# Fused recurrence and two expert mixtures: low parts of the first mixture's weights by an accumulating transfer

## The chip, the cores and the metric

The kernel runs on one core of a Trainium2 chip. Its engines work side by side: TensorE (PE in the profile; PEld is its weight load), VectorE (DVE), ScalarE (ACT), GpSimd (POOL) and SyncE (SP, which issues most transfers). The metric is the device time in microseconds (us), the median of several runs. For the kernel before it is 1308.95 us (three runs, 1308.48 to 1310.84).

## What is computed

```python
def reference(**kwargs):
    attn_out = _attn_ref(**attn_kwargs)          # a gated linear recurrence over 2 x 5056 tokens of 256
    x = attn_out.reshape(B * S, D)               # 10112 tokens
    x = _moe_ref(x=x, **moe_kwargs)              # first mixture
    return _moe2_ref(x=x, **moe2_kwargs)         # second mixture

def _moe_ref(x, w_gate, w1, w2):                 # 8 experts, each takes exactly N // 8 = 1264 tokens
    ...                                          # pairs (token, expert) taken greedily by their logit
    for e in range(E):
        mask = assigned == e
        h = np.maximum(x[mask] @ w1[e], 0.0)     # 256 -> 1024
        out[mask] = h @ w2[e]                    # 1024 -> 256

def _moe2_ref(x, expert_emb, tau, w1, w2):       # 8 experts, each token goes to its best one
    ...
        out[mask] = gate_w[mask, None] * (h @ w2[e])
```

The matrix products are done in a short float format (`fp32r`). So that the result is precise enough, each operand is split into a high part (the value rounded to that format) and a low part (the value minus its high part), and each product is the sum of three: high by high, high by low, low by high.

## The kernel before

**Stages.** The recurrence fills the first 180 us or so. The first mixture follows, to about 800 us: eight *phases*, one for each expert in the order in which the greedy assignment fills them. The second mixture takes the rest, in blocks of 512 and 256 tokens.

**A phase** has five chunks of up to 256 tokens and four *steps* for each chunk, so 20 steps. A step is `g1` (first layer for two of the eight groups of 128 hidden units, PE lines L1125) and, two steps later, `g2` (second layer, L1157 to L1159). Between them ACT writes the high part `hh` (L1130) and DVE the low part `hl` (L1131). Each chunk's tokens come by two GpSimd indirect transfers, the gathers `xg` (L1092), and PE turns them (`L1100`) before ACT and DVE split them.

**Work beside the steps of a phase** prepares the next one: the *selection* of the next expert and its tokens, a long chain of small DVE operations with a few on ACT and PE. Two of its places matter here. `lists` (L943 to L970) turns the chosen tokens into a list of numbers: DVE writes `om` (L953), `oh` (L957), `lo` (L959) and `rh` (L960, L961), then PE does 24 small products (L966), and from their result come the numbers `ids` that the gathers use. The search for the cut uses `KY` (L222, turned on PE at L769) and counts `scm` on ACT (L794). POOL also adds third parts of results (L1201) and stores rows by indirect transfers (`x2r`, L1266).

**The weights** of the next phase come as four raw tiles of 128x1024 numbers (512 KB each, issued by SP). `split_weights` makes of each a high part on ACT (L1055) and a low part: where `low[k]` is V, by one DVE subtraction (L1057), where it is G, by four POOL subtractions of 128x256 (L1063). Phase 0 has V four times, phase 1 has V, G, V, G, phases 2 to 7 have G four times, the first block of the second mixture has G, V, G, V, all later blocks have V.

**What sets the order.** Every engine works through its own instructions in the order in which the program wrote them. That order comes from a planner, the class `Flow`: each job is a generator that yields a cost for each engine (`{"A": 0.95, "G": 2.6}`) and a delay. The planner keeps a clock for each engine and writes a job's next piece when, by these costs, its engine will be free. PE sets the pace. `fl.until(...)` runs the planner until a job is done by its clock. A changed cost therefore moves instructions of all engines, in the whole first mixture.

Of the kernel before, what the change touches and what calls it, by code (L numbers as in the profile page):

```python
# [9 lines left out]
F32 = mybir.dt.float32  # L10
# [3 lines left out]
AF = mybir.ActivationFunctionType  # L14
ALU = mybir.AluOpType
# [5 lines left out]
D = 256  # L21
# [33 lines left out]
W_FIRST = 5.0  # L55
# [26 lines left out]
def build(tc, x, r_gate, i_gate, a_param, w_gate, w1, w2, emb, tau, v1, v2, out):  # L82
    nc = tc.nc
    V, A, G, T, SP = nc.vector, nc.scalar, nc.gpsimd, nc.tensor, nc.sync
# [4 lines left out]
    def ct(name, shape, dt=F32):  # L89
        return cp.tile(shape, dt, name=name)  # L90
# [122 lines left out]
    fl = Flow()  # L213
# [204 lines left out]
    low, top = ct("low", [P, 1]), ct("top", [P, 1])  # L418
# [623 lines left out]
    def split_weights(raw, low, wt, first=0.0, each=0.0):  # L1042

        wt.update({n: wp.tile([P, 2, F], F32R, name=n) for n in ("w1h", "w1l")})
        wt.update({n: wp.tile([P, NF, D], F32R, name=n) for n in ("w2h", "w2l")})
        for k in range(4):
            while len(raw) <= k:
                yield {}, 0.1
            yield {"A": 0.95, **({"G": 2.6} if low[k] is G else {"V": 1.13})}, each if k else first
            if k < 2:  # L1050
                src, h, l = raw[k], wt["w1h"][:, k], wt["w1l"][:, k]
            else:
                src = raw[k].rearrange("p (f d) -> p f d", d=D)
                h, l = (wt[n][:, 4 * k - 8:4 * k - 4, :D] for n in ("w2h", "w2l"))
            A.activation(h, src, AF.Copy)  # L1055
            if low[k] is V:
                V.tensor_tensor(out=l, in0=src, in1=h.bitcast(F32), op=ALU.subtract)  # L1057
                continue

            for q in range(4):  # L1060
                at = slice(q * D, (q + 1) * D)
                p = (lambda t: t[:, at]) if k < 2 else lambda t: t[:, q]
                G.tensor_tensor(out=p(l), in0=p(src), in1=p(h.bitcast(F32)), op=ALU.subtract)  # L1063


    base = ct("base", [P, E])
# [6 lines left out]
    st = {ph: dict(x={}, xg=[], w={}) for ph in range(E)}  # L1073
# [9 lines left out]
    def gather(ph, c):  # L1083
        o = st[ph]
        ids = sel[ph]["ids"]
        t0, n = CHUNKS[c]
        xg = room(o, "xg", [P, 2, D], bufs=XG)
        o["xg"].append(xg)
        for j in range((n + P - 1) // P):
            yield dict(G=1.04), 0  # L1090
            k = t0 // P + j
            G.indirect_dma_start(out=xg[:, j], out_offset=None, in_=x1,  # L1092
                                 in_offset=bass.IndirectOffsetOnAxis(ap=ids[:, k:k + 1], axis=0),
                                 bounds_check=N - 1, oob_is_err=False)
        yield {}, 3.0
# [176 lines left out]
    def load_of(ph):  # L1272
        e = nc.values_load(sel[ph]["ei"], engines=[ENG.SP], min_val=0, max_val=E - 1,
                           skip_runtime_bounds_check_because="one of the eight experts")
        st[ph]["raw"] = []
        return load_weights(st[ph]["raw"], w1, w2, e)
# [5 lines left out]
    fl.until(("lists", 0))  # L1282
    t = fl.free["PE"]
    sp0 = split_weights(st[0]["raw"], [V, V, V, V], st[0]["w"])
    drain(gather(0, 0))
    fl.done.add(("g", 0, 0))
# [14 lines left out]
    def poll(ph, u):  # L1301

        nonlocal loaded
        for p in range(2, E):
            if p <= ph + 2 and ("ei", p - 1) in fl.done and ("sel", p) not in chain:
                chain["sel", p] = 1
                fl.add(PRIO_SEL, ("sel", p), select(p, sp, pm))
        p = ph + 1
        if p < E:
            if ("ei", p) in fl.done and ("w", p - 1) in fl.done and loaded < p:  # L1310
                loaded = p
                fl.add(2, ("load", p), load_of(p))
            if loaded == p and u >= 2 and ("w", p) not in chain:
                chain["w", p] = 1
                fl.add(4, ("w", p), split_weights(st[p]["raw"], [V, G, V, G] if p == 1 else [G, G, G, G], st[p]["w"], W_FIRST))
            if ("lists", p) in fl.done:
                for c in range(NCH):

                    k = c + NCH - XG
                    if ("g", p, c) not in chain and (k < 0 or ("x", ph, k) in fl.done) and (c == 0 or ("g", p, c - 1) in chain):  # L1320
                        chain["g", p, c] = 1
                        fl.add(4 if c > 0 else 2.5, ("g", p, c), gather(p, c))

        if ("base", E - 2) in fl.done and "early" not in chain:
            chain["early"] = 1
            fl.add(1, "early", early())
    def early():

        yield from table("e")
        B[0] = {}  # L1330
        yield from b_raw(0)
        o = B[0]
        o["w"] = {}
        fl.add(4, ("w", E), split_weights(o["raw"], [G, V, G, V], o["w"], 4.0, 1.5))
        while ("route", E - 2) not in fl.done:
            yield {}, 0.1
        yield {}, 3.0
        while "again" not in fl.done:
            yield {}, 0.1
        placed.extend(last_rows)  # L1340
        b_rows(0)
        B[1] = {}
        yield from b_raw(1)
# [6 lines left out]
    def tick(ph, u):  # L1350
        poll(ph, u)
        fl.run()
# [59 lines left out]
    nE, nI, nbk, cum, first = bt("nE", [1, E]), bt("nI", [1, E], I32), bt("nbk", [1, E]), bt("cum", [1, E]), bt("first", [1, E])  # L1412
# [248 lines left out]
    for u in range(NU):  # L1661
# [13 lines left out]
        if f == 2 and c == NCH - 1 and ph + 1 < E:  # L1675
            while ("g", ph + 1, 0) not in fl.done:
                poll(ph, u % NB)
                fl.run(0.2)
            fl.add(1, ("x", ph + 1, 0), x_part(ph + 1, 0))
# [125 lines left out]
```

## Time and profile before

| | |
|---|---|
| median of three runs | 1308.95 us |
| the profiled execution: its own time, its span | 1319.5 us, 1317.8 us |
| PE busy, share of the span | 1154.1 us, 88% |
| DVE busy | 891.7 us, 68% |
| ACT busy | 691.7 us, 52% |
| POOL busy | 421.7 us, 32% |

The profiled execution is 10.6 us longer than the median. The profile names an instruction by its line, its engine and its operands (`out<-in`), and for an engine's idle time it names what ended it, the releaser. PEclk is the clock that TensorE was granted, as a share of full speed.

### The profile page before, as it was taken

The numbers are of one execution on the slowest core, as the hardware profiler recorded it, in microseconds if no ns is written. First come the engines' busy times: TensorE is split into PE (matmuls) and PEld (weight loads), VectorE is DVE, ScalarE is ACT, GpSimd is POOL, SyncE is SP. The second block draws the span as 40 slices with busy tenths as digits, with TensorE's granted clock in tenths as the row PEclk, the third lists the DMA queues.
The fourth block names the chain that finished last, engine by engine and source line by source line (L and its number), as shares of the span: only waits on it lengthen the run. The fifth ranks groups of instructions, "written<-read, shape, count | busy, mean of one in ns | idle before, by whom it ended". The sixth has DMA issues, their size and how long they took to land. (4 is left out here: it accounts for less than half of the span.)

```text
span 1317.8 us, 24375 instructions
## 1 busy us (share of the span) xinstructions
PE 1154.1 (88%) x9051; PEld 1087.3 (83%) x9051; DVE 891.7 (68%) x2014; ACT 691.7 (52%) x1188; POOL 421.7 (32%) x514
## 2 busy tenths in 40 slices
PE   5666669898888979788899898889999999999997
PEld 3544569798888979788899897779999999999996
DVE  5799876767594776846843345856666667887883
ACT  7999745453535444443344335434444445666663
POOL 1000030515546272543756042231212122212222
PEclk9668679898889998879899898989999999999998
DMA  9765561415243242434244166858555544999991
GB/s 314 245 209 179 193 227 25 120 34 153 58 117 99 71 121 61 126 76 122 74 131 114 27 159 146 217 171 234 154 167 147 168 117 136 232 226 240 246 237 41
DMA packets 250500, 195.48 MB, mean 148 GB/s; under 512 B 150198, under 2 KB 231775, under 8 KB 250368
## 3 DMA queue, kind: packets, MB, share of 16 engines
q1 hardware_dynamic: 236528, 157.00, 44.3%
q0 software_dynamic: 12992, 36.76, 8.7%
q8 instruction: 76, 1.25, 0.4%
q14 instruction: 56, 0.46, 0.1%
q10 hardware_dynamic: 848, 0.03, 0.0%
HBM read 121.65 MB, written 40.68 MB: 123 GB/s over the span
## 5 line engine op out<-in xcount | busy, mean ns | idle before, releaser
L1130 ACT ACTIVATE hh<-pa 128x512 fp32r<-128x512 f32 (+1 forms) x232 | 137.2, 592 | 304.5 <-PE pa L1125 239.9
L1131 DVE SCALAR_TENSOR_TENSOR hl<-pa,hh 128x512 fp32r<-128x512 f32 (+1 forms) x232 | 158.2, 683 | 173.5 <-ACT hh L1130 159.1
L1632 POOL DMA_INDIRECT out_dram<-br,xw x84 | 106.6, 1269 | 345.5 <-ACT br L1623 326.9
L1125 PE MATMUL pa<-xh,w1h 128*128 128x256 f32 (+1 forms) x928 | 195.8, 293 | 8.8 <-DVEq L1694 5.7
L1157 PE MATMUL px<-w2h,hh 128*128 128x256 f32 (+1 forms) x640 | 195.6, 306 | 1.4 <-issue 1.4
L1125 PE MATMUL pa<-xl,w1h 128*128 128x256 f32 (+1 forms) x928 | 191.9, 289 | 3.9 <-issue 2.4
L1125 PE MATMUL pa<-xh,w1l 128*128 128x256 f32 (+1 forms) x928 | 191.3, 288 | 1.3 <-DVE l L1211 0.7
L1158 PE MATMUL px<-w2l,hh 128*128 128x256 f32 (+1 forms) x640 | 187.8, 293 | 3.0 <-issue 3.0
L1159 PE MATMUL px<-w2h,hl 128*128 128x256 f32 (+1 forms) x640 | 187.5, 293 | 1.0 <-issue 1.0
L1125 PEld LDWEIGHTS pa<-xh,w1h 128*128 128x128 f32 x928 | 149.4, 198 | 10.6 <-issue 9.2
L1125 PEld LDWEIGHTS pa<-xl,w1h 128*128 128x128 f32 x928 | 149.3, 198 | 5.7 <-issue 3.4
L1125 PEld LDWEIGHTS pa<-xh,w1l 128*128 128x128 f32 x928 | 149.4, 198 | 0.8 <-issue 0.8
L1159 PEld LDWEIGHTS px<-w2h,hl 128*128 128x128 f32 (+1 forms) x640 | 128.3, 200 | 3.1 <-issue 3.1
L1157 PEld LDWEIGHTS px<-w2h,hh 128*128 128x128 f32 (+1 forms) x640 | 128.5, 201 | 2.4 <-issue 2.2
L1158 PEld LDWEIGHTS px<-w2l,hh 128*128 128x128 f32 (+1 forms) x640 | 128.5, 201 | 1.9 <-issue 1.8
L1201 POOL TENSOR_TENSOR big<-br,big 128x256 bf16<-128x256 f32 x80 | 54.0, 695 | 230.3 <-ACT big L1198 230.3
L1596 ACT ACTIVATE hh<-pa 128x512 fp32r<-128x512 f32 x96 | 57.1, 597 | 132.4 <-PE pa L1593 129.5
L1266 POOL DMA_INDIRECT x2r<-big,de x80 | 82.5, 1032 | 72.6 <-issue 44.3
L1597 DVE SCALAR_TENSOR_TENSOR hl<-pa,hh 128x512 fp32r<-128x512 f32 x96 | 66.0, 687 | 55.9 <-ACT hh L1596 55.3
L1092 POOL DMA_INDIRECT xg<-x,ids x80 | 83.3, 1041 | 43.7 <-DMA raw<-in_moe_w_dram 21.1
L1612 PE MATMUL px<-w2h,hh 128*128 128x256 f32 x336 | 94.9, 282 | 0.5 <-ACT big L1198 0.5
L1614 PE MATMUL px<-w2h,hl 128*128 128x256 f32 x336 | 95.1, 283 | 0.0
(385 smaller groups left out, 2854.1 us busy)
## 6 DMA issues: line engine op xcount, KB each, us to landing
raw<-in_moe_w_dram SPq DMA_DIRECT2D x92, 512.0 KB
big<-in_moe_w_dram SPq DMA_DIRECT2D x60, 512.0 KB
hT<-in_r_gate_dram SPq DMA_DIRECT2D x38, 256.0 KB
it<-in_i_gate_dram SPq DMA_DIRECT2D x19, 512.0 KB
xt<-in_x_dram SPq DMA_DIRECT2D x19, 512.0 KB
x<-xr SPq DMA_DIRECT2D x11, 512.0 KB
x<-it SPq DMA_DIRECT2D x8, 512.0 KB
x2r<-KT SPq DMA_DIRECT2D x8, 393.0 KB
```

The costliest lines, as they stand in the source:

```text
L1092: G.indirect_dma_start(out=xg[:, j], out_offset=None, in_=x1, in_offset=bass.IndirectOffsetOnAxis(ap=ids[:, k:k + 1], axis=0), bounds_chec ...
L1125: T.matmul(pa[:, q * n:(q + 1) * n], a[:, kc, fs], b[:, kc, :n], start=(k == 0), stop=(k == 5))
L1130: A.activation(hh[:, :2 * n], pa[:, :2 * n], AF.Relu)
L1131: V.scalar_tensor_tensor(hl[:, :2 * n], pa[:, :2 * n], 0.0, hh[:, :2 * n].bitcast(F32), op0=ALU.max, op1=ALU.subtract)
L1157: T.matmul(px, hh[:, ts], w["w2h"][:, f], start=(f == 0 and a == 0), stop=False)
L1158: T.matmul(px, hh[:, ts], w["w2l"][:, f], start=False, stop=False)
L1159: T.matmul(px, hl[:, ts], w["w2h"][:, f], start=False, stop=(f == NF - 1 and a == 1))
L1266: i = G.indirect_dma_start(out=x2r, out_offset=bass.IndirectOffsetOnAxis(ap=de[:, j:j + 1], axis=0), in_=rw[:, j, :], in_offset=None, boun ...
L1597: V.scalar_tensor_tensor(hl, pa, 0.0, hh.bitcast(F32), op0=ALU.max, op1=ALU.subtract)
L1612: T.matmul(px, hh[:, ts], w["w2h"][:, f, :D], start=(f == 0 and a % 2 == 0), stop=False)
L1614: T.matmul(px, hl[:, ts], w["w2h"][:, f, :D], start=False, stop=(f == NF - 1 and a % 2 == 1))
L1632: i = G.indirect_dma_start(out=out, out_offset=bass.IndirectOffsetOnAxis(ap=o["g"][:, a, E:].bitcast(I32), axis=0), in_=ot[a // 2][:, a % ...
```

## The change

Where POOL had made a low part by four subtractions, ACT now writes minus the high part into the low part's place (an activation with scale -1, which rounds as the one for the high part does), and POOL issues one transfer of the raw tile that adds to what stands there. Phase 1 now does this for all four tiles, so that its two DVE subtractions go too. In all that is 30 low parts: four in each of phases 1 to 7 and two in the first block of the second mixture. The planner's costs follow, and a job with such low parts is done only 5 us, by its clock, after its last piece.

```diff
@@ split_weights
-            yield {"A": 0.95, **({"G": 2.6} if low[k] is G else {"V": 1.13})}, each if k else first
+            yield ({"A": 1.95, "G": 1.1} if low[k] is G else {"A": 0.95, "V": 1.13}), each if k else first
             ...
             A.activation(h, src, AF.Copy)
             if low[k] is V:
                 V.tensor_tensor(out=l, in0=src, in1=h.bitcast(F32), op=ALU.subtract)
-                continue
-
-            for q in range(4):
-                at = slice(q * D, (q + 1) * D)
-                p = (lambda t: t[:, at]) if k < 2 else lambda t: t[:, q]
-                G.tensor_tensor(out=p(l), in0=p(src), in1=p(h.bitcast(F32)), op=ALU.subtract)
+            else:
+
+                A.activation(l, src, AF.Copy, scale=-1.0)
+                G.dma_start(out=l.bitcast(F32), in_=src, accum_op=ALU.add)
+        if G in low:
+            yield {}, 5.0
@@ poll
-                fl.add(4, ("w", p), split_weights(st[p]["raw"], [V, G, V, G] if p == 1 else [G, G, G, G], st[p]["w"], W_FIRST))
+                fl.add(4, ("w", p), split_weights(st[p]["raw"], [G] * 4, st[p]["w"], W_FIRST))
```

In the changed kernel L1060 is ACT's new write and L1061 POOL's transfer.

**POOL, end of phase 0**, where the weights and the first gathers of phase 1 are prepared. Before:

```order
L1063 TENSOR_TENSOR w1l<-raw,w1h 128x256 x4
L1092 DMA xg<-x_85,ids 128x256 x3
L1063 TENSOR_TENSOR w2l<-raw,w2h 128x256 x4
L1201 TENSOR_TENSOR big_1988<-br,big_1988 128x2x128 x2
L1092 DMA xg<-x_85,ids 128x256 x7
```

and now:

```order
L1061 DMA w1l<-raw 128x1024 x2
L1061 DMA w2l<-raw 128x1024
L1092 DMA xg<-x_85,ids 128x256 x2
L1061 DMA w2l<-raw 128x1024
L1201 TENSOR_TENSOR big_1988<-br,big_1988 128x2x128 x2
L1092 DMA xg<-x_85,ids 128x256 x8
```

The first two gathers now stand behind the third low part, where before they stood behind one.

**POOL, end of phase 5**, where phase 6 is prepared. Before:

```order
L1063 TENSOR_TENSOR w1l<-raw,w1h 128x256 x4
L1266 DMA x2r<-big_6370,de 96256x393
L1092 DMA xg<-x_85,ids 128x256
L1063 TENSOR_TENSOR w2l<-raw,w2h 128x256 x4
L1201 TENSOR_TENSOR big_7491<-br,big_7491 128x2x128 x2
L1092 DMA xg<-x_85,ids 128x256
L1063 TENSOR_TENSOR w2l<-raw,w2h 128x256 x4
L1092 DMA xg<-x_85,ids 128x256 x5
```

and now:

```order
L1061 DMA w1l<-raw 128x1024
L1266 DMA x2r<-big_6316,de 96256x393
L1061 DMA w2l<-raw 128x1024
L1266 DMA x2r<-big_6316,de 96256x393
L1061 DMA w2l<-raw 128x1024
L1266 DMA x2r<-big_6316,de 96256x393
L1092 DMA xg<-x_85,ids 128x256
L1266 DMA x2r<-big_6316,de 96256x393
L1092 DMA xg<-x_85,ids 128x256
```

Both gathers of phase 6's first chunk stood ahead of the last low part; now they stand behind it, with a row store between each.

**ACT, the same place.** The activation L1106 at the end is the split of phase 6's first chunk, and each L1130 is one step. Before:

```order
L1055 ACTIVATE w2h<-raw 128x1024
L1130 ACTIVATE hh<-pa 128x480 x2
L1185 ACTIVATE big_7491<-px 128x2x2x128
L1189 ACTIVATE jk,ss_7493<-px 128x256 x2
L1130 ACTIVATE hh<-pa 128x480
L1198 ACTIVATE big_7491<-br 128x2x2x128
L1106 ACTIVATE xh<-tp 128x512
```

and now:

```order
L1055 ACTIVATE w2h<-raw 128x1024
L1060 ACTIVATE w2l<-raw 128x1024
L1185 ACTIVATE big_7397<-px 128x2x2x128
L1189 ACTIVATE jk,ss_7399<-px 128x256 x2
L1130 ACTIVATE hh<-pa 128x480
L1198 ACTIVATE big_7397<-br 128x2x2x128
L1106 ACTIVATE xh<-tp 128x512
```

The last high part had three steps between itself and the first chunk of phase 6; now it and the new write have one.

## Rows read from the trace of the kernel before

**Rows 1.** Busy time by stretch: PE, PEld, DVE, ACT, POOL, then granted clock, DMA, GB/s.
```profile
375.00:450.00 75.00, 64.19 (x545) 62.17 (x545) 49.25 (x136) 35.10 (x78) 39.50 (x48) 0.91 0.35 98
```

**Rows 2.** PE's waits, 200 to 850 us: releaser, total us, times, longest.
```profile
PE sm L966 <- DVE rh L961: 20.5, 5, 6.4
...
PE tp L769 <- DVE KY L222: 2.5, 1, 2.5
```

**Rows 3.** PE's timeline, every waiting L966: start, duration, instruction, [idle before, releaser].
```profile
242.06 0.77 PE L966 MATMUL sm<-rh,lo 128*128 128x20 bf16 x24 [1.09 <-DVE rh L961]
...
391.80 0.80 PE L966 MATMUL sm<-rh,lo 128*128 128x20 bf16 x24 [5.91 <-DVE rh L961]
...
466.08 0.76 PE L966 MATMUL sm<-rh,lo 128*128 128x20 bf16 x24 [4.37 <-DVE rh L961]
...
550.99 0.80 PE L966 MATMUL sm<-rh,lo 128*128 128x20 bf16 x24 [6.39 <-DVE rh L961]
...
634.58 0.81 PE L966 MATMUL sm<-rh,lo 128*128 128x20 bf16 x24 [2.72 <-DVE rh L961]
```

**Rows 4.** DVE's timeline before the wait at 242.06, POOL idle.
```profile
240.84 0.16 DVE L953 SCALAR_TENSOR_TENSOR om<-hif,flg 128x1 f32<-128x1 bf16 x1
240.92 0.40 DVE L957 TENSOR_TENSOR oh<-hif,ib 128x240 bf16<-128x240 bf16 x1
```

**Rows 5.** Timelines of DVE and POOL before the wait at 391.80.
```profile
384.71 3.35 DVE L953 SCALAR_TENSOR_TENSOR om<-hif,flg 128x1 f32<-128x1 bf16 x1
...
385.25 2.79 POOL L1063 TENSOR_TENSOR w1l<-raw,w1h 128x256 fp32r<-128x256 f32 x4
```

**Rows 6.** Timelines of DVE and POOL before the wait at 550.99.
```profile
546.98 3.28 DVE L957 TENSOR_TENSOR oh<-hif,ib 128x240 bf16<-128x240 bf16 x1
...
547.22 2.77 POOL L1063 TENSOR_TENSOR w2l<-raw,w2h 128x256 fp32r<-128x256 f32 x4
...
550.15 1.00 POOL L1266 DMA_INDIRECT x2r<-big,de  x1 [0.17 <-issue]
...
550.54 0.39 DVE L961 TENSOR_TENSOR rh<-oh,vb 128x240 bf16<-128x240 bf16 x1
```

**Rows 7.** Short stretches behind four of these waits: PE busy, granted clock, DMA, GB/s.
```profile
242.00:246.00 4.00, 3.94 (x62) 1.00 0.71 247
392.00:396.00 4.00, 4.00 (x52) 0.59 0.00 0
...
551.00:555.00 4.00, 4.00 (x49) 0.50 0.15 54
635.00:641.00 6.00, 6.00 (x42) 0.50 0.41 139
```

**Rows 8.** Groups by line: count, busy us, mean ns, idle before, releasers.
```profile
L1130 ACT ACTIVATE hh<-pa 128x512 fp32r<-128x512 f32 (+1 forms) x232 | 137.2, 592 | 304.5 <-PE pa L1125 239.9 <-remote 33.7 <-issue 12.2
...
L1055 ACT ACTIVATE w2h<-raw 128x1024 fp32r<-128x1024 f32 x46 | 48.5, 1055 | 1.6 <-DMA raw<-in_moe_w_dram 1.5
...
L1063 POOL TENSOR_TENSOR w2l<-raw,w2h 128x256 fp32r<-128x256 f32 x56 | 42.3, 788 | 15.4 <-ACT w2h L1055 15.3
```

**Rows 9.** Timelines of ACT and PE, start of phase 6's first chunk.
```profile
652.93 0.57 ACT L1130 ACTIVATE hh<-pa 128x480 fp32r<-128x480 f32 x1 [2.37 <-PE pa L1125]
...
656.91 0.65 PE L1100 MATMUL tp<-ident,xg 128*128 128x128 f32 x4
```

**Rows 10.** Timelines of POOL and PE, start of phase 1's first chunk.
```profile
248.19 1.00 POOL L1092 DMA_INDIRECT xg<-x,ids  x1 [0.30 <-issue]
...
252.76 0.90 PE L1100 MATMUL tp<-ident,xg 128*128 128x128 f32 x3 [2.54 <-DMA xg<-x,ids]
```

**Rows 11.** ACT's timeline while four raw tiles of 512 KB land in turn.
```profile
183.76 1.06 ACT L1055 ACTIVATE w2h<-raw 128x1024 fp32r<-128x1024 f32 x1 [0.42 <-DMA raw<-in_moe_w_dram]
185.27 1.06 ACT L1055 ACTIVATE w2h<-raw 128x1024 fp32r<-128x1024 f32 x1 [0.46 <-DMA raw<-in_moe_w_dram]
```

**Rows 12.** POOL's timeline, the longest issue of a transfer from 400 to 800 us.
```profile
466.77 1.60 POOL L1266 DMA_INDIRECT x2r<-big,de  x1 [0.16 <-issue]
```

## The prediction

> **What bounds the kernel now.** I first read busy time by stretch, to see which engine has the least room in the stage that changes. In a stretch of one phase, 375 to 450 us, PE is busy for 64.2 of 75 us, DVE for 49.3, POOL for 39.5, ACT for 35.1 [rows 1]. PE sets the pace, but 10.8 us of the stretch it is idle, and its clock is 0.91 of full on average. So I read next what PE waits for: the largest releaser is DVE's `rh` ahead of the small products L966, 20.5 us in five waits; `KY` adds one of 2.5 us [rows 2]. The selection, then, a side job on DVE, holds PE up; the reader should ask why DVE is late there although it is busy for only two thirds of the time.
>
> The timelines answer. Of the five waits, that at 242.06 is 1.09 us and the others 5.91, 4.37, 6.39 and 2.72 us [rows 3]. Ahead of the short one POOL stands idle, and DVE's `om` takes 0.16 us and `oh` 0.40 us [rows 4]. Ahead of that at 391.80 the same `om` takes 3.35 us and ends as POOL's four subtractions for a low part end, 385.25 + 2.79 = 388.04 [rows 5]. Ahead of that at 550.99 `oh` takes 3.28 us and lasts until the four subtractions of another low part end, 547.22 + 2.77 = 549.99; the `rh` that then runs beside POOL's issue of an indirect transfer takes 0.39 us [rows 6]. A small DVE operation that meets POOL's subtractions is held until they are over; beside the issue of a transfer it is not. I take this as the reason for the four long waits.
>
> PE also pays afterwards. Behind the 1.09 us wait its clock stays at 1.00, behind three of the long ones the stretches stand at 0.59, 0.50 and 0.50, the last at the lower of its two levels, 1.2 of 2.4 GHz, throughout [rows 7].
>
> **The change part by part.** POOL loses 28 x 4 = 112 subtractions of 0.79 us [rows 8], 88 us, and gains 30 issues; an issue costs 1.00 us [rows 6] and the gap behind one 0.30 us [rows 10], so 39 us. POOL does not bound, so the difference by itself is worth nothing. What counts is that these subtractions no longer hold DVE.
>
> *The waits at L966.* If each of the four long waits falls to the 1.09 us of the one that POOL left alone, the saving is 5.91 + 4.37 + 6.39 + 2.72 - 4 x 1.09 = 15.0 us. Ends: only the excess of the two operations of over 3 us goes, 3.19 + 2.88 = 6.1 us, or all of the waits, 19.4 us. I take 15.0, since the row for it is the same code with the suspect absent.
>
> *The wait at KY.* It stands in the same chain, and I count 2 of its 2.5 us; ends 0 and 2.5.
>
> *The clock.* In the stretches of rows 7 a PE that was busy all the time lost 4 x 0.41 + 4 x 0.50 + 6 x 0.50 = 6.6 us; the fourth wait, at 466.08, I put at the smallest of the three, 1.6 us. Together 8.3 us (with rounding), all of it gone if short waits leave the clock alone, as the first row of rows 7 has it; the other end is 0.
>
> *ACT's new writes.* 30 activations of 1.055 us [rows 8] are 31.7 us. ACT has room: before its 232 `hh` it idles for 304.5 us, 1.3 us each [rows 8], a little more than one new write, and PE asks for `hh` only two steps later. I charge 2 us where several stand in a row; ends 0 and 31.7. If the cover were gone, all of them would count, since PE's second layer waits for `hh` and `hl`.
>
> *The planner's new order.* Two places cost something. At the end of phase 0 the gathers for phase 1 now stand behind the third low part on POOL, which cannot be issued before ACT has written it: two more writes, 2.1 us. PE already waits there for the gather [rows 10], so this goes on top: 2.1 us.
>
> At the end of phase 5 it is more. The last high part follows the `hh` that ends at 652.93 + 0.57 = 653.5 [rows 9]. Two activations bring ACT to 655.6. POOL then issues the last low part, a store, a gather, a store, a gather: five times 1.3 us, 662.1. From the end of a gather's issue to PE's use the trace has 252.76 - 249.19 = 3.6 us [rows 10], which gives 665.7. PE wanted the chunk at 656.91 [rows 9], so it waits for 8.8 us, where before it did not. Ends: 0, if PE comes that much later or a gather lands sooner, and 8.8 plus the transfers ahead of it in POOL's queue, up to 4.5 us each (below). I take 8.8. In the other phases the gathers have two steps or more behind the last low part, and I charge nothing.
>
> *The transfer itself.* The trace has no adding transfer. From below: raw tiles of the same size that stream in land 185.27 - 183.76 = 1.5 us apart [rows 11]. From above: two reads and a write in turn, 4.5 us. I take two of three, 3.0 us; what follows on POOL's queue waits behind it. It is hidden wherever steps lie between the last low part and its use; without that cover each phase would begin 3 us late, 21 us in seven phases. The Trainium skill (Collectives: The Full Stack, the section on the bandwidth ceiling) says that an adding transfer is slower because it reads two sources, which halves the rate of a copy. By that rule a low part takes 3.0 us here and the sum stays; no row of this trace shows it.
>
> *The rest.* Two DVE subtractions of phase 1 go; PE does not wait for them, so nothing. The 5 us that the planner adds move only its own marks; the order in which this results is counted above.
>
> **Sum.** 15.0 + 2.0 + 8.3 - 2.0 - 2.1 - 8.8 = 12.4 us saved. The profiled execution took 1319.5 us for a span of 1317.8; 12.4 less is 1307.1. It stands 10.6 us above the median of 1308.95, and in the same ratio the forecast is 1309 - 12.3, about **1296 us**.
>
> **The rivals.**
> *All cover holds*: as forecast, but PE's wait at phase 6 is hidden and ACT costs nothing. Then 1309 - 23 = 1286, and with the upper end of the waits 1279. For it: the planner often has PE arrive later than in the old order. Against: the row store and gather order on POOL is plain.
> *The wait moves*: the selection is one chain, and PE meets it again at `KY` and at the counts; only the two blocks of over 3 us are saved, 6.1 us, with their clock, 4 x 0.41 + 4 x 0.50 = 3.6, less the costs of 12.9: 1312. For it: PE follows the chain step by step in a fixed order. Against: DVE is busy for only two thirds of the stretch.
> *Slower, the transfers stand ahead of the gathers*: gathers go through the same queue of POOL. If in the four phases in which they follow closely (1, 2, 4 and 6) two adding transfers are still under way, each phase's start moves by 2 x 3.0 = 6 us, 24 us in all: 1320. It decides from 12.4 / 4 = 3.1 us in each, that is from about one transfer in the way. Against: ACT needs over 2 us for each pair of writes, and the four low parts are spread over several steps.
> *POOL's issues are held by DVE*: the longest issue in the second half of the mixture took 1.60 us against 1.00 [rows 12]; four such delays of 0.6 us ahead of the gathers of those four phases give 9.6 us: 1306. The Trainium skill (SBUF — State Buffer, Who interferes with whom) speaks against the change here: transfers that GpSimd issues can starve while VectorE holds the port that their descriptors need. By that rule the time would be this rival's; the trace agrees as to the kind, with 0.6 us.
> *The change doesn't do what it says*: DVE is held by the new issues as by the subtractions. Then only the costs are left, 1309 + 12.9 = 1322. Against: the 0.39 us of `rh` beside an issue [rows 6].
>
> **How the numbers follow.** Forecast (1288 to 1304) 0.44; all cover holds 0.17; the wait moves 0.17; transfers ahead of the gathers 0.14; held issues 0.05; not as said 0.03. A measurement of this kernel can tell about 0.2%, 2.6 us. Faster by more (below 1306.3): 0.44 + 0.17 + half of the held issues + 0.02 of the moved wait, 0.65. Within 0.2%: the other half and 0.10 of the moved wait, 0.13. Slower: the rest, 0.22. The range goes from 1279, where all terms stand at their good ends, to 1318, inside the slower rival, and leaves out under 2 in 10.
>
> **What would show it.** Right: `om`, `oh`, `lo` and `rh` near their times of rows 4 in every phase; the waits of L966 near 1 us and no clock of 0.5 behind them; a new wait of PE for `xg` of 5 us or more at the start of phase 6, and a longer one at phase 1. ACT's L1060 at 30 x 1.055 us. Wrong: PE's waits for DVE of the old size at other lines of the selection; PE waiting for a transfer at the first L1125 of a phase, which would mean that an adding transfer takes far longer than 4.5 us; POOL issues of several us; or PE waits for `hh`.

## The result, and the profile after

The changed kernel takes 1326.54 us (median of 8 runs, 1319.09 to 1327.93) against 1309.91 us for the kernel before on the same chip: a ratio of 1.0117, interval 1.0091 to 1.0143. It is 1.2% slower. The forecast was 1296 us and faster, and 1326.5 us lies outside its range. Its profiled execution took 1322.6 us for a span of 1320.5, a little under its median, while that of before was above its own, so the two profiles show less than the difference of the medians.

PE's waits of the changed kernel from 200 to 850 us (releaser, total us, times, longest) answer to [rows 2]:

```profile
PE tp L769 <- DVE KY L222: 12.1, 3, 10.1
PE sm L1209 <- DMA bt<-big: 11.2, 6, 4.4
PE sm L905 <- DVE gt L888: 10.7, 1, 10.7
...
PE tp L1100 <- DMA xg<-x,ids: 3.7, 2, 2.0
PE sm L966 <- DVE rh L961: 3.2, 4, 2.4
```

What the change was made of did happen: the waits at L966 fell from 20.5 to 3.2 us. In their place stand one wait of 10.1 us at `KY`, one of 10.7 us at `gt`, both further up the same selection chain, and 11.2 us at `bt`, a turn of rows by SP's transfers. The two DVE operations that were held, grouped by line (minimum, median, longest ns), are not held any more (the hold by POOL's subtractions is called the lock below); in [rows 5, 6] single ones took 3.35 and 3.28 us:

```profile
L953 DVE SCALAR_TENSOR_TENSOR om<-hif,flg x8: 159/159/161, 178.1 to 652.6; 128x1 f32<-128x1 bf16 x8
...
L957 DVE TENSOR_TENSOR oh<-hif,ib x8: 396/401/403, 178.1 to 652.7; 128x240 bf16<-128x240 bf16 x8
```

The two long waits are alike. The first, near the end of phase 0, from the timelines of SP, ACT, DVE and PE (start, duration, instruction, [idle before, releaser]):

```profile
241.08 1.13 SPq L1036 DMA_DIRECT2D raw<-in_moe_w_dram  x2
...
245.93 1.06 ACT L1055 ACTIVATE w1h<-raw 128x1024 fp32r<-128x1024 f32 x1 [5.89 <-DMA raw<-in_moe_w_dram]
246.89 1.04 ACT L1060 ACTIVATE w1l<-raw 128x1024 fp32r<-128x1024 f32 x1
...
248.42 0.66 DVE L1131 SCALAR_TENSOR_TENSOR hl<-pa,hh 128x480 fp32r<-128x480 f32 x1 [5.62 <-ACT hh L1130]
...
256.01 2.24 DVE L222 SCALAR_TENSOR_TENSOR KY<-scrA,Mc 128x640 f32<-128x640 f32 x1
...
258.31 1.11 PE L769 MATMUL tp<-ident,KY 128*128 128x128 f32 x4 [10.06 <-DVE KY L222]
```

Read it downwards. ACT stands at a high part and waits 5.89 us for its raw tile. The next `hh` is queued behind the two writes on ACT, `hl` behind that `hh` on DVE, the selection's `KY` behind `hl`, and PE comes to `KY` 10.06 us before it is there. A part of this is not the raw tile's: `KY` itself took 2.24 us here, against a median of 0.82 us, beside two subtractions that POOL still does (L1201, 255.87 to 257.56). The second, near the end of phase 5:

```profile
623.45 0.87 SPq L1036 DMA_DIRECT2D raw<-in_moe_w_dram  x1
...
632.43 1.06 ACT L1055 ACTIVATE w2h<-raw 128x1024 fp32r<-128x1024 f32 x1 [6.82 <-DMA raw<-in_moe_w_dram]
633.39 1.04 ACT L1060 ACTIVATE w2l<-raw 128x1024 fp32r<-128x1024 f32 x1
...
636.28 0.66 DVE L1131 SCALAR_TENSOR_TENSOR hl<-pa,hh 128x480 fp32r<-128x480 f32 x1 [8.30 <-ACT hh L1130]
...
640.70 0.86 DVE L888 SCALAR_TENSOR_TENSOR gt<-Mc,vs,q 128x80 f32<-128x80 f32 x1
...
641.62 0.19 PE L905 MATMUL sm<-ng,oneb 128*128 128x1 bf16 x1 [10.71 <-DVE gt L888]
```

Here the raw tile is not there 8 us after its issue has ended. Two things could make that so: the new order, which puts the splits closer behind the loads, and the adding transfers, if they hold up the load on the DMA engines. The queue of transfers that POOL issues (packets, MB, share of 16 engines' span) grew from 12992 packets, 36.76 MB, 8.7% to:

```profile
q0 software_dynamic: 17312, 52.49, 15.6%
```

That is (15.6% x 1320.5 - 8.7% x 1317.8) / 30 = 3.0 us of all 16 engines for each transfer.

Stretches behind L966 and behind the two new waits answer to [rows 7] (us, busy PE, PEld, DVE, ACT, POOL, then granted clock, DMA share, GB/s):

```profile
319.00:323.00 4.00, 4.00 (x42) 4.00 (x43) 2.71 (x5) 3.00 (x6) 1.93 (x2) 0.58 0.97 215
391.00:395.00 4.00, 4.00 (x54) 4.00 (x53) 1.53 (x5) 2.49 (x3) 0.90 (x1) 1.00 1.07 271
464.50:468.50 4.00, 4.00 (x62) 4.00 (x62) 1.25 (x2) 3.74 (x8) 1.16 (x2) 1.00 1.03 308
...
258.00:262.00 4.00, 2.82 (x12) 2.44 (x12) 1.81 (x7) 2.48 (x6) 3.21 (x3) 0.50 1.20 182
641.50:647.50 6.00, 5.35 (x30) 5.30 (x30) 4.33 (x21) 0.60 (x1) 4.92 (x6) 0.58 0.74 156
```

Behind the short L966 waits at 391 and 464 the clock stays at 1.00, as forecast; behind the wait of 2.42 us at 319 and behind the two new ones it is at or near its lower level. The clock's loss moved with the waits.

### The profile page after: what moved, and what is told of

Same layout as the page of the kernel before. It is cut to its first block, busy times and chain, and to the rows that moved or that the text cites. A ratio compares the mean times of both kernels' runs of the same rounds, so it can differ in the third digit from the quotient of the medians.

```text
span 1320.5 us, 24358 instructions
## 1 busy us (share of the span) xinstructions
PE 1144.2 (87%) x9051; PEld 1079.4 (82%) x9051; DVE 857.2 (65%) x2012; ACT 717.9 (54%) x1218; POOL 369.5 (28%) x432
## 3 DMA queue, kind: packets, MB, share of 16 engines
q0 software_dynamic: 17312, 52.49, 15.6%
## 5 line engine op out<-in xcount | busy, mean ns | idle before, releaser
L1130 ACT ACTIVATE hh<-pa 128x512 fp32r<-128x512 f32 (+1 forms) x232 | 137.1, 592 | 274.9 <-PE pa L1125 208.3
L1201 POOL TENSOR_TENSOR big<-br,big 128x256 bf16<-128x256 f32 x80 | 54.0, 707 | 250.3 <-ACT big L1198 250.2
```

What stands on the lines that cost most here:

```text
L1130: A.activation(hh[:, :2 * n], pa[:, :2 * n], AF.Relu)
```

## The experiments

Each ratio is to the kernel before in the same set of runs. In the sets of `e1` to `e4` and of `e10` to `e13` the kernel before took 1268 us, in all others 1309 to 1311; two ratios compare safely only where the kernel before took the same. Three theories stood at the start: **A**, the planner's new order is the price; **B**, ACT's second write is; **C**, the adding transfers are.

**Two halves of the change.** `e1_old_order` makes the transfers under the old prices, list and order (PE and DVE in before's order); `e2_new_order` takes the new order and leaves the low parts to POOL's subtractions.

```
e1: yield {"A": 0.95, **({"G": 2.6} ...)}; no "yield {}, 5.0"; [V, G, V, G] if p == 1
    A.activation(l, src, AF.Copy, scale=-1.0)
    G.dma_start(out=l.bitcast(F32), in_=src, accum_op=ALU.add)
e2: yield ({"A": 1.95, "G": 1.1} ...); "yield {}, 5.0"; [G] * 4
    G.tensor_tensor(out=p(l), in0=p(src), in1=p(h.bitcast(F32)), op=ALU.subtract)   # four times
```

> The low parts by ACT's write and the adding transfer, but with the planner's old costs and the old list for phase 1, so that every engine's other instructions stand as before the change. Theory A (the planner's new order is what costs: it puts the selection and the weights where ACT and the gathers meet them late): 1290 to 1300 us, since the waits at L966 go and nothing comes in their place. Theory B (ACT's second write, in line with the steps and behind raw tiles that land late): about 1318 us, as the changed kernel or a little less. Theory C (the adding transfers hold up the raw tiles and the turned tiles on the DMA engines): about 1318 us too.

> The new order alone: the planner's new costs and lists as in the changed kernel, but the low parts by POOL's subtractions. Theory A: 1325 us or more, slower than the changed kernel, since DVE is held by POOL as well. Theories B and C: about 1310 us, as the kernel before.

Measured: `e1_old_order` 1.0049 (1.0029 to 1.0069), `e2_new_order` 1.0163 (1.0133 to 1.0192). So the order alone, with the subtractions kept, costs no less than the whole change did, and the transfers in the old order gain nothing although the waits at L966 are gone there too (3.8 us). With the order's price in hand, what ate the gain in `e1_old_order` is the next question.

**The transfer taken out of the new order, or made plain.** `e3_no_transfer` drops the transfer, so that minus the high parts stand for the low parts; `e4_copy` makes it a copy of the raw tile, so that the raw weights stand there. The data that follow are other than the kernel's.

```
e3: -                G.dma_start(out=l.bitcast(F32), in_=src, accum_op=ALU.add)
e4: +                G.dma_start(out=l.bitcast(F32), in_=src)
```

> The changed kernel without its 30 adding transfers: the low parts stay at minus the high parts, so the products are not the reference's. All else stands in the same order. Theory C: 1300 us or less, the whole loss gone. Theory B: 1322 us. Theory A: 1322 us, at most the gathers' share of some 5 us less.

> The changed kernel with its 30 transfers as plain copies of the raw tile (the sum is left out, so the low parts are the raw weights). Same order, same issues on POOL; each packet reads one source and not two. Theory C: half of what taking the transfers out gains, about 1312 us. Theories A and B: 1324 us, no change.

Measured: 1.0237 (1.0213 to 1.0260) and 1.0092 (1.0065 to 1.0119). The first can't be read as it stands: with its outputs of the first mixture the second one routes differently (240 `hh` instead of 232), and everything behind the first mixture's last `hh` takes 547 us instead of the 514 to 520 us of the other kernels. From the first to the last `hh` of the first mixture it took 555.1 us, with copies 568.9 us. That speaks for C, but the data differ between the two, so the trial was made again with data that differ less.

**The square, and two other ways to write the low parts.** `e6_after` is the changed kernel in the set of the three others. `e7_dve_low` keeps before's order and has DVE write all low parts. `e8_old_zero` (old order) and `e9_new_zero` (new order) keep ACT's second write but let it write zeros, without any transfer; the small low parts are left out of the products.

```
e7:      V.tensor_tensor(out=l, in0=src, in1=h.bitcast(F32), op=ALU.subtract)
e8, e9:  A.activation(l, src, AF.Copy, scale=0.0)          # and no dma_start
```

> The changed kernel as it is, on the chip of the runs beside it. All theories: 1.2% over before (ratio 1.009 to 1.014), since nothing differs from the run that gave the result. It is the fourth corner of the square of orders and low parts: old order with subtractions (before), old order with transfers (1.005), new order with subtractions (1.016), new order with transfers (this).

> Before's planned order of all engines, with the low parts written by VectorE instead of GpSimd: no subtractions of GpSimd, no transfers, no second write of ScalarE. Theory A with C (the lifted lock is worth some 15 us, the transfers and the new order each eat it): about 34 us of subtractions (30 of 1.13 us, VectorE's price for one in the planner's table) come onto VectorE, which is busy two thirds of the span; if half of them find it idle and the rest stand in the selection chain, the net lies at -15 + 17, ratio 0.99 to 1.01. Rival B (ScalarE's second write makes the loss): the second write is gone, so 0.985 to 0.99.

> Before's planned order, ScalarE's second write kept but writing zeros, no adding transfers and no subtractions of GpSimd; the low parts of the first mixture's weights are left out of the computation. Theory C (the transfers take the DMA engines): the gain of the lifted lock shows, 12 to 20 us under the old order with transfers, ratio to before 0.988 to 0.995. Rival B (ScalarE's second write, and not the transfer, is the price): as the old order with transfers, 1.003 to 1.007.

> The changed kernel with ScalarE's second write kept but writing zeros and without the adding transfers; the low parts of the first mixture's weights are left out of the computation. Its output stays close to the reference, so the second mixture routes as in the changed kernel and whole times compare. Theory A with C: the new order keeps its price of some 15 to 20 us, the transfers' 14 to 20 us go: 1262 to 1270 us here, ratio 0.997 to 1.003. Rival A alone (transfers are free, the order is all): as the changed kernel, 1.010 to 1.014. Rival C alone (the order is free, the transfers are all): as the old order without transfers, 0.988 to 0.995.

Measured: `e6_after` 1.0101 (1.0069 to 1.0132), `e7_dve_low` 0.9912 (0.9880 to 0.9944), `e8_old_zero` 0.9886 (0.9853 to 0.9919), `e9_new_zero` 0.9962 (0.9933 to 0.9990). Theory A with C holds in both orders: without transfers the lifted lock is worth 1.1%, with ACT's second write in it, and the transfers take 1.6% (old order) or 1.4% (new). The 1.4% is read within one set; the 1.6% joins `e1_old_order` and `e8_old_zero` from two, and the next experiments give 1.7% within one, against a plain copy. A alone and C alone are out. B is out as the main cause: the second write is in `e8_old_zero`. And `e7_dve_low`, which leaves nothing out, beats both kernels.

The new order's own marks are seen in `e9_new_zero`, where no transfer is in the way (PE's timeline, its two largest waits of the first seven phases; in `e8_old_zero` neither place has a wait above 2.5 us):

```profile
256.46 1.12 PE L769 MATMUL tp<-ident,KY 128*128 128x128 f32 x4 [6.16 <-DVE KY L222]
...
635.04 0.18 PE L905 MATMUL sm<-ng,oneb 128*128 128x1 bf16 x1 [9.18 <-DVE gt L888]
```

They are the two places of the changed kernel, at 6.16 and 9.18 us in place of 10.06 and 10.71: the waits belong to the order, and come out longer with the transfers. ACT's wait for a raw tile is only a part of them: 3.75 us in front of `KY` and 2.73 us in front of `gt` in this trace. The rest is work that stands in line behind the split; from the start of that high part at 625.41 to the end of `gt` at 634.97 ACT and DVE are at work for 9.6 us without a pause of note.

**What of a transfer costs.** All three in the old order: `e10_add_high` adds the high part instead of the raw tile, so that the raw tile is free early; `e11_half_add` adds half as much; `e12_zero_copy` moves as much by a plain copy.

```
e10: G.dma_start(out=l.bitcast(F32), in_=h.bitcast(F32), accum_op=ALU.add)     # onto minus the high part
e11: G.dma_start(out=a.bitcast(F32), in_=b.bitcast(F32), accum_op=ALU.add)     # a, b: the halves of l, zeros
e12: G.dma_start(out=l.bitcast(F32), in_=l.bitcast(F32))                       # zeros
```

> Old order with transfers, but each transfer adds the high part, and not the raw tile, to minus the high part, so that the low parts come out as zeros and are left out of the computation; the raw tile is free as soon as ScalarE has read it. Theory C1 (the time that the transfers take of the DMA engines is the price): the same bytes in the same packets, so as the old order with transfers, 1.003 to 1.007. Rival C3 (the raw tile is held until the transfer has landed, so the next load is issued late and ScalarE waits for it): the hold is gone, as the old order without transfers, 0.986 to 0.992.

> Old order, ScalarE writes zeros as low parts and a transfer of half the size adds one half of these zeros to the other; the low parts are left out of the computation. Theory C1: half of the transfers' price of 1.6% stays, ratio 0.995 to 0.999. Rival C3: 0.986 to 0.992, since the transfer doesn't touch the raw tile. Rival C4 (a fixed price for each transfer, its issue or its start, whatever its size): as with whole transfers, 1.003 to 1.007.

> Old order, ScalarE writes zeros as low parts and a plain copy of whole size moves them onto themselves; the low parts are left out of the computation. Theory C1 with the durations of packets (327 ns for one of an adding transfer, about 170 ns for a plain one): half of the price of 1.6%, ratio 0.995 to 0.999. Rival (bytes count, adding or not): 1.003 to 1.007.

Measured: 1.0060 (1.0035 to 1.0085), 0.9924 (0.9904 to 0.9943), 0.9886 (0.9858 to 0.9914). Holding the raw tile is not the price, and zeros as data don't make a kernel faster, since `e10_add_high` has them too. Against the whole plain copy half an addition costs 0.4% (the intervals overlap), a whole one 1.7%, all in one set. The copy stands at the ratio of `e8_old_zero`, which has no transfer but is from a set at 1310 us, so that it is free in this order is likely and not shown. So it isn't a price for each transfer, nor one for each byte, and it isn't proportional to the DMA time that follows either. The queue's rows for `e8_old_zero` (no transfers), `e10_add_high`, `e11_half_add` and `e12_zero_copy`, in this order:

```profile
q0 software_dynamic: 12992, 36.76, 8.8%
```

```profile
q0 software_dynamic: 17024, 51.44, 15.3%
```

```profile
q0 software_dynamic: 17024, 44.10, 12.4%
```

```profile
q0 software_dynamic: 17024, 51.44, 12.2%
```

With the spans of 1297.6, 1273.0, 1255.7 and 1253.4 us, 28 transfers of each kind took 2.9 us of all engines for a whole addition, 1.5 for half of one and 1.4 for a copy. The Trainium skill (Collectives: The Full Stack, the section on the bandwidth ceiling) says of the steps of a ring collective that one that adds runs at half the rate of a copy, since it reads two sources; the traces agree for these transfers, 2.9 against 1.4 us.

Where the time is met can be read at one place, the load that is issued in phase 3, where SP issues the last two of the four raw tiles (those of w2) and ACT's high part waits for the first of them. Without transfers:

```profile
460.56 1.10 SPq L1036 DMA_DIRECT2D raw<-in_moe_w_dram  x2
...
465.33 1.06 ACT L1055 ACTIVATE w2h<-raw 128x1024 fp32r<-128x1024 f32 x1 [2.33 <-DMA raw<-in_moe_w_dram]
```

With plain copies:

```profile
444.65 1.03 SPq L1036 DMA_DIRECT2D raw<-in_moe_w_dram  x2
...
449.63 1.06 ACT L1055 ACTIVATE w2h<-raw 128x1024 fp32r<-128x1024 f32 x1 [2.59 <-DMA raw<-in_moe_w_dram]
```

With half additions:

```profile
447.05 1.09 SPq L1036 DMA_DIRECT2D raw<-in_moe_w_dram  x2
...
452.93 1.06 ACT L1055 ACTIVATE w2h<-raw 128x1024 fp32r<-128x1024 f32 x1 [3.50 <-DMA raw<-in_moe_w_dram]
```

With whole additions:

```profile
449.96 0.87 POOL L1061 DMA_DIRECT2D w1l<-w1h  x1 [0.94 <-ACT w1l L1060]
451.05 2.35 SPq L1036 DMA_DIRECT2D raw<-in_moe_w_dram  x2
...
460.67 1.06 ACT L1055 ACTIVATE w2h<-raw 128x1024 fp32r<-128x1024 f32 x1 [8.20 <-DMA raw<-in_moe_w_dram]
```

From the start of SP's issue to ACT's start it is 4.8, 5.0, 5.9 and 9.6 us. The whole addition for a part of w1 was issued 1.1 us ahead of the load, the half addition 0.1 us ahead and the plain copy 0.3 us behind it, so the four places are alike but not the same.

**Is that the price?** If it is (theory C2), only w1's transfers cost, since w2's loads stand behind them. `e14_w1_dve` has DVE write w1's low parts and keeps the transfers for w2; `e15_w2_dve` is its mirror.

```
e14: -            if low[k] is V:
     +            if low[k] is V or k < 2:
e15: +            if low[k] is V or k >= 2:
```

> Old order with transfers, but the low parts of an expert's two w1 tiles (k below 2) are written by VectorE, those of the two w2 tiles by the adding transfer; nothing is left out. Theory C2 (the transfers' price is paid where w1's adding transfers run beside the raw loads of w2 that stand behind them, so that ScalarE waits for raw tiles before it splits w2): ScalarE's waits for raw tiles fall from some 26 us to about 11, as without transfers, and the ratio is 0.986 to 0.993. Rival (the DMA time of the adding transfers as such, wherever they run): half of the price of 1.6% stays, 0.996 to 1.000.

> The mirror of the run beside it: old order, w1's low parts by the adding transfer, w2's by VectorE; nothing is left out. Theory C2: ScalarE's waits for raw tiles of w2 stay at 15 to 20 us and with them most of the price, ratio 0.999 to 1.005. Rival (DMA time as such): half of the price, 0.996 to 1.000, as its mirror.

Measured: 0.9937 (0.9916 to 0.9959) and 0.9948 (0.9924 to 0.9971). ACT's waits for raw tiles, 190 to 800 us, came as C2 says; first `e14_w1_dve`, then `e15_w2_dve`:

```profile
ACT w1h L1055 <- DMA raw<-in_moe_w_dram: 6.3, 2, 5.0
ACT w2h L1055 <- DMA raw<-in_moe_w_dram: 3.7, 3, 2.5
```

```profile
ACT w2h L1055 <- DMA raw<-in_moe_w_dram: 14.9, 3, 7.9
ACT w1h L1055 <- DMA raw<-in_moe_w_dram: 6.2, 2, 4.8
```

But 11 us less of waiting is worth 1.4 us of time by the ratios (3.2 us by the medians), and the intervals overlap. C2 falls as the whole account: the longest row in the trace is where the transfers are seen, and only a part of what they cost. The rival asked for 0.996 to 1.000, and both ratios lie below that. Against `e7_dve_low`, half of the transfers with their writes cost 0.2 to 0.4%, all of them (`e1_old_order`, from a set at 1268 us) 1.4%. Together with `e11_half_add` this says that the price grows faster than the DMA time; that half of it finds room and the second half doesn't is the reading that fits, and no trace shows it directly.

Where PE pays can be read from the pair of one set, `e12_zero_copy` and `e10_add_high`, between the first and the last `hh` of the first mixture, which hold the same work (stretch, its length, then busy PE, PEld, DVE, ACT, POOL, granted clock, DMA share, GB/s; below each PE's waits in that stretch):

```profile
191.70:735.60 543.90, 512.58 (x4683) 505.93 (x4683) 346.57 (x1076) 294.18 (x622) 220.99 (x265) 0.97 0.49 133
...
PE tp L769 <- DVE KY L222: 5.5, 4, 2.0
PE tp L1098 <- ACT KT L770: 3.7, 1, 3.7
...
PE sm L1207 <- DMA bt<-big: 1.3, 2, 0.9
```

```profile
190.70:755.60 564.90, 521.14 (x4684) 513.54 (x4683) 348.08 (x1076) 294.37 (x621) 230.51 (x265) 0.95 0.54 127
...
PE tp L769 <- DVE KY L222: 9.2, 4, 4.2
PE tp L1098 <- ACT KT L770: 6.8, 1, 6.8
...
PE sm L1207 <- DMA bt<-big: 3.9, 3, 2.1
```

Of the 21.0 us, PE is busy for 8.6 us more, at a lower clock, and idle for 12.4 us more, of which 3.7 at `KY`, 3.1 at `KT` (the next link of the selection, written by ACT) and 2.6 at `bt`, the turns by SP. In the new order the turns are the largest part: from 200 to 850 us PE waits for `bt` 1.9 us in `e9_new_zero`, 7.1 us with the plain copies of `e16_new_copy` (next experiment) and 11.2 us in the changed kernel (19.6 us in the trace of `e6_after`).

```profile
PE sm L1208 <- DMA bt<-big: 1.9, 4, 1.0
```

```profile
PE sm L1209 <- DMA bt<-big: 7.1, 5, 3.1
```

So besides the loads SP's turns are held up. How much of the waits at `KY` and `KT` comes from late raw tiles was not told apart.

**Plain copies in the new order.** `e16_new_copy` puts the copy of `e12_zero_copy` into the new order.

```
+                A.activation(l, src, AF.Copy, scale=0.0)
+                G.dma_start(out=l.bitcast(F32), in_=l.bitcast(F32))
```

> New order, ScalarE writes zeros as low parts, and a plain copy of whole size moves them onto themselves; the low parts are left out of the computation. In the old order this copy cost nothing (0.9886 with and without it), but plain copies of the raw tile in the new order gave 1.0092, against 0.9962 without transfers. Theory C1 (a plain copy is short enough to be hidden in either order; what the copy of the raw tile cost was its hold on the tile): 0.994 to 0.999. Rival (the new order splits right behind the loads, so it has no room even for a plain copy): 1.005 to 1.011.

Measured: 1.0000 (0.9983 to 1.0017), between the two expectations: 0.4% above `e9_new_zero`, its interval touching that one's. The new order seems to have less room than the old. The 1.0092 of `e4_copy` is not explained by this; it differs in holding the raw tile, in its data and in the set (1268 us before), and which of them it was wasn't told apart.

**The order.** `e13_all_dve` is `e7_dve_low` with the planner told of it, so that it plans an order of its own. `e17_reroll` changes nothing but one price in the planner's table. `e19_new_dve` writes the low parts by DVE in the changed kernel's order.

```
e13: -  [V, G, V, G] if p == 1 else [G, G, G, G]
     +  [V] * 4
e17: -  yield {"A": 0.95, **({"G": 2.6} if low[k] is G else {"V": 1.13})}, each if k else first
     +  yield {"A": 0.95, **({"G": 2.5} if low[k] is G else {"V": 1.13})}, each if k else first
e19: -  A.activation(l, src, AF.Copy, scale=-1.0)
     -  G.dma_start(out=l.bitcast(F32), in_=src, accum_op=ALU.add)
     +  V.tensor_tensor(out=l, in0=src, in1=h.bitcast(F32), op=ALU.subtract)
```

> Before with all low parts written by VectorE, and the planner told so (1.13 us each of VectorE's time, none of GpSimd's), so that it makes an order of its own. Against the run with VectorE's low parts in the old order (0.991). Theory A (a new order of this planner is worth a per cent more or less by itself): anything from 0.982 to 1.003. Rival (an order planned with true costs is the better one): below 0.991.

> Before with one number of the planner's changed, the price of GpSimd's subtractions 2.5 instead of 2.6 us, which changes nothing that is computed or issued, only the order that is planned. Theory A as it stands now (before's order is a good draw, and any new order of this planner pays for it): slower, 1.003 to 1.016. Rival (the new order of the changed kernel is bad for a reason of its own, its prices of ScalarE's and GpSimd's work): within 0.998 to 1.002.

> The changed kernel's order with the low parts by VectorE, no second write of ScalarE and no transfers; nothing is left out. It gives the price of the new order with neither subtractions of GpSimd nor transfers in the way, beside 0.991 for the same low parts in the old order. Theory (the three prices add: lifted lock -1.1%, transfers 1.4%, order 0.6 to 1.0%): 0.996 to 1.002. Rival (the order's price came of the lock or the transfers that it collides with): 0.988 to 0.993.

Measured: 1.0032 (1.0017 to 1.0048), 1.0097 (1.0068 to 1.0126), 0.9969 (0.9946 to 0.9991). A price of 2.5 for 2.6, with the same instructions, makes the kernel 1.0% slower. From 190 to 800 us its largest wait in total is the old one, and its longest single one is new, at the same line, with no releaser that the trace names:

```profile
PE sm L966 <- DVE rh L961: 18.5, 5, 5.9
...
PE sm L966 <- issue: 6.9, 1, 6.9
```

So a new order can be worse without the change's mechanism; whether that of the changed kernel is worse for a reason of its own is left open. All three new orders lose to the old one: 1.0 (`e17_reroll`), 1.2 (`e13_all_dve` against `e7_dve_low`, from two sets) and 0.6% (`e19_new_dve` against it). Three draws don't show how often one would win.

**ACT's second write by itself.** `e18_dve_and_write` is `e7_dve_low` with the write kept ahead of DVE's subtraction, which overwrites it.

```
+                A.activation(l, src, AF.Copy, scale=-1.0)
                 V.tensor_tensor(out=l, in0=src, in1=h.bitcast(F32), op=ALU.subtract)
```

> Old order, low parts by VectorE as in the run of 0.991, but ScalarE's second write (minus the high part) is kept ahead of it and overwritten; nothing is left out. It prices the write by itself: 28 writes of 1.04 us come back onto ScalarE, and VectorE's subtraction stands about 1 us later. My theory (the write is nearly free, ScalarE is busy 53% and waits for TensorE): 0.991 to 0.995. Rival B (the write is on ScalarE's path to the next high part and a fair part of the loss): 0.996 to 1.003.

Measured: 1.0014 (0.9998 to 1.0030), 1.0% more than without the write. By the numbers expected that would be rival B, but DVE's waits (190 to 800 us) show that the trial doesn't price ACT alone:

```profile
DVE w2l L1061 <- ACT w2l L1060: 12.2, 7, 3.6
DVE w1l L1061 <- ACT w1l L1060: 9.6, 7, 3.3
```

DVE now stands waiting for the second write, 21.8 us against 10.5 us at `e7_dve_low`'s two lines, with the selection queued behind. In the changed kernel only POOL waits for that write. What it costs there stays open: `e8_old_zero` shows only that the lifted lock and the write together gain 1.1%, and a lock worth more with a dearer write would give the same.

The runs in one table, ratios to before:

| low parts by | old order | new order |
|---|---|---|
| POOL's subtractions | 1 (before) | 1.0163 |
| ACT's write and adding transfer | 1.0049 | 1.0117, 1.0101 (the change) |
| ACT writes zeros, plain copy | 0.9886 | 1.0000 |
| ACT writes zeros, no transfer | 0.9886 | 0.9962 |
| DVE's subtractions | 0.9912 | 0.9969 |

Down a column is what the way of writing costs, across a row what the order costs. Only steps between runs of one set are safe. `e8_old_zero`, `e9_new_zero` and `e6_after` are of one set and lead from before to the change: lock and write -1.14%, order +0.76%, transfers +1.39%, together the 1.01% of `e6_after`. Such a path adds up by construction; what it shows is the size of each step.

## Why the prediction was wrong, point by point

- **The waits at L966, -15.0 us: right.** 20.5 us became 3.2 us. The reason was right too, since DVE's `om` and `oh` are at their times of [rows 4] in all eight of their runs.
- **`KY`, -2 us: wrong in sign.** It rose to 12.1 us. `e9_new_zero` has 9.8 us of it without any transfer, so the most of that is the order's.
- **The clock, -8.3 us: not got.** The clock did stay at 1.00 behind two short L966 waits, but fell behind the new waits; the mean over the span went from 0.918 to 0.914. The term took the waits' loss of clock as gone, without asking what the new waits would cost in clock.
- **The whole gain.** Lock, clock and ACT's write were put at 25.3 - 2 = 23.3 us. `e8_old_zero` has just these three in before's order, and gains 1.14% or 15 us. The term was half as large again as it should have been; which of the three was off wasn't told apart.
- **ACT's writes, 2 us: not contradicted, not priced.** They take 1.045 us each in the trace. `e18_dve_and_write` doesn't tell.
- **The order, +10.9 us: the size near, the places wrong.** Across the table it costs 0.5 to 0.8%, 7 to 10 us, in the rows of adding transfers, no transfer and DVE (1.6 and 1.1% in the other two; the rows of adding transfers and of copies join two sets). But PE's waits for `xg` fell (4.7 to 3.7 us), at phase 6 there is none, and the two gather waits that made up the 10.9 us are not there. The order is paid at `KY` and `gt`, where splits that stand close behind the loads make ACT wait and the selection stands in line behind them. That wait is in none of the prediction's terms.
- **The transfer, 0 us: this is the step that failed.** Its length was right, 2.9 to 3.0 us against an estimate of 3.0. What was wrong is "hidden wherever steps lie between the last low part and its use": that asks when the low part is needed, and not who else needs the DMA engines while it is made. Their price is 1.4 to 1.7%, 18 to 22 us, more than the whole gain of 12.4 us that was forecast; PE paid it in waits at `KY`, `KT` and `bt` and in clock. The prediction's bad end for this term, 21 us, has that size by luck: it stood for seven phases that begin late for want of a low part, and no wait of PE for a low part is in the list of the changed kernel. The sum with the measured steps of one set, -15 for lock, clock and write, +10 for the order and +18 for the transfers, is 13 us slower, 1323; measured were 1324 and 1327.
- **The rivals.** "Transfers stand ahead of the gathers" gave 1320, near the time by luck, with the wrong mechanism: `xg` waits did not grow. "Issues held by DVE": the longest of the 30 new issues took 1.02 us, and the longest of a gather or a store from 190 to 830 us 1.55 us, against 1.60 before. So nothing new was held. Whether DVE makes those long issues, as the Trainium skill (SBUF — State Buffer, Who interferes with whom) has it for transfers that GpSimd issues, no run here shows. "The change doesn't do what it says" is out by L957's row above. "The wait moves" was right in kind: PE did meet the chain again at `KY`, though by new causes.

## What to carry to other kernels

A transfer that replaces work on an engine is not free because its result is needed late: count its time on the DMA engines, and look which loads and turns are in flight beside it and who waits for them in order. Half of the traffic may be free and the other half dear, so try a smaller share before all of it. Where a planner sets the order, change the mechanism and the planner's numbers one at a time: here one price changed by 4% cost 1.0%, about what the lifted lock was worth. And when an engine is held by another, the direct way out may be to let the held one do the work: 28 more subtractions on DVE, 1.22 us each, made the fastest complete kernel, 0.9912 of before.

## What the runs showed of the hardware

- An adding transfer of 512 KB between tiles takes 2.9 us of all 16 DMA engines, a plain copy 1.4 us; the issue takes POOL 0.95 us for an addition and 0.58 us for a copy, by the groups of L1061 in `e10_add_high` and `e12_zero_copy`:

```profile
L1061 POOL DMA_DIRECT2D w1l<-w1h x14: 869/954/1012, 244.6 to 740.2; - x14
```

```profile
L1061 POOL DMA_DIRECT2D w1l<-w1l x14: 545/576/606, 245.7 to 721.4; - x14
```

- At the one place read, the first of two raw tiles issued 1.1 us behind such an addition reached its user 9.6 us after the issue began, against 4.8 us with none about. Loads and additions are on different queues; a queue of its own did not spare the load.
- The price of adding transfers on the time is not linear: 0.4% at half the size and 1.7% at full size over the plain copy, in the same order of all engines.
- The kernel before took 1268 us in two sets of runs and 1309 to 1311 us in the others, 3.4% apart, and one chip's number stands beside both levels (1310.3 and 1268.3 us, under half an hour apart). The gap lies in the first mixture: from its first to its last `hh` the kernels took 543 to 578 us in the sets at 1268 us and 589 to 618 us in the others, and 514 to 520 us behind it in both (547 in `e3_no_transfer`). In every trace at the higher level PE stands for 13.6 to 24.1 us between 190 and 800 us with no releaser that the trace knows ("issue"), at the lower level never. What sets the level stays open.
